# A long-convolution prologue: filter sums moved in place to GpSimd, unit sums moved to VectorE, weight conversion begun earlier, and a reordered group loop

## The chip, the cores and the metric

The kernel runs on one core of a Trainium2 chip. The metric is the device time of one execution in microseconds (us), lower being better. Each kernel was run several times, and its median is given with the lowest and the highest run. All executions quoted here are in the fast state: none is over 1.5% above the fastest of its kernel. A profile shows a single one of these executions, and executions differ by some microseconds among themselves.

## The reference, cut to what matters

```python
# B=4, S=12544, D=128, DFF=768
h_filt = (np.maximum(pos_emb @ w1, 0.0) @ w2) * window      # perceptron that makes the filter
u = x * v
y = irfft(rfft(u, 2*S) * rfft(h_filt, 2*S))[:, :S]          # long convolution along the sequence
x = (x * y).reshape(B * S, D)
h = np.maximum(np.maximum(x @ moe_w1, x @ moe_w2), x @ moe_w3)   # moe weights arrive as float64
return h @ moe_w_out
```

The Fourier transforms are done as matrix products in three stages.

## The kernel before

The program has a prologue of some 412 us and a main loop of some 2090 us. The main loop (the other three batches, the inverse transform and the feed-forward products) is bound by TensorE and is not touched. The prologue has these stages:

1. A perceptron makes the filter's taps (to 44.8 us). ScalarE, VectorE and TensorE work in turn.
2. The filter's first transform, 16 "quads" (44.8 to 69.3 us).
3. The first transform of batch 0, in 16 pairs of "units" (69.3 to about 179 us). Each unit is a product `ut = x*v`, four transposes, a quad of 32 matmuls, and a sum and a difference of its two planes.
4. A loop over 45 groups (about 184 to 379 us). Each step makes one part of the filter's spectrum (`s_second`, copied to G, then `s_filter`, copied to `ht`), multiplies it with the spectrum of batch 0, transforms back (`g_third`), and stores the tile `zs` to DRAM.
5. A hand-over to the main loop.

Two jobs run beside stage 3. The float64 weights are turned into float32 by 96 integer steps on VectorE ("conversion steps"), and the filter's own sums over its two planes are made.

```python
def over_w(ps, dst, tmp):                # sums of a unit: ScalarE copies one plane, VectorE sums
    v = by_r(ps)
    nc.scalar.copy(tmp, v[:, :, 1, :])
    for c, op in enumerate((ALU.add, ALU.subtract)):
        nc.vector.tensor_tensor(out=dst[:, :, c, :].rearrange("p k s -> p s k"), in0=tmp,
                                in1=v[:, :, 0, :], op=op)          # in1 is in PSUM

def over_w_there(ps, dst, tmp):          # the same with the sums on GpSimd
    v = by_r(ps)
    nc.scalar.copy(tmp, v[:, :, 1, :])
    d0, d1 = (dst[:, :, c, :].rearrange("p k s -> p s k") for c in range(2))
    nc.scalar.copy(d0, v[:, :, 0, :])
    nc.gpsimd.tensor_tensor(out=d1, in0=tmp, in1=d0, op=ALU.subtract)
    nc.gpsimd.tensor_tensor(out=d0, in0=tmp, in1=d0, op=ALU.add)

def filter_over_w(k):                    # sums of the filter, five blocks a call
    s0, s1, t = specH[:, k:k + 5, 0], specH[:, k:k + 5, 1], misc[:, 0:5 * FO].rearrange(...)
    nc.gpsimd.tensor_tensor(out=t, in0=s1, in1=s0, op=ALU.subtract)
    nc.gpsimd.tensor_tensor(out=s0, in0=s1, in1=s0, op=ALU.add)
    nc.scalar.copy(s1, t)

for u in range(0, NU, 2):                # the pairs of units; NU = 32
    t = uts.pop(u)
    for v in range(2):
        if u + 4 < NU:
            u_mul(u + 4 + v)             # ut = x*v on VectorE
        at = 4 * (u + v)
        quad([t[:, 4 * v + i] for i in range(4)], f1[:], spec[:, :, :, at:at + 4],
             over_w_there if (u + v) % 5 in (1, 3) else over_w)
        if at < 4 * N1 // 5:
            filter_over_w(5 * at // 4)
        some(1)                          # one conversion step
    if u + 4 < NU:
        turn2(u + 4)                     # transposes of a later pair, copied to uT by ScalarE
    ...                                  # loads of later units
    some(2)

# ---- the loop over groups; NK = 45
def g_pair(g):
    dt = zss[g]
    zs = cvp.tile([P, 2, 2, D], FP32, tag="z", name="zs", bufs=2)
    for a, op in enumerate((ALU.add, ALU.subtract)):
        nc.vector.tensor_tensor(out=zs[:, a], in0=dt[:, 0:2, :], in1=dt[:, 2:4, :], op=op)
    zss[g] = zs

def g_store(b, g):                       # 256 KB, issued by GpSimd
    nc.gpsimd.dma_start(zd[b][2 * g:2 * g + 2].rearrange(...), zss.pop(g)[:].rearrange(...))

for s in range(-1, NK + 5):              # conditions on s at the ends are cut
    s_filter(s)                          # TensorE from G; ScalarE copies to ht
    g_second(s)                          # TensorE: spectrum of the data
    g_swap(s)                            # ScalarE: xs
    g_re(s)                              # VectorE: xt
    s_second(s + 1)                      # TensorE, then ScalarE copies to G (two buffers)
    g_turn(s - 3)                        # ScalarE on dt
    g_third(s - 2)                       # TensorE: transform back, reads table wi
    wi[s] = load_dir(s, 1)               # 256 KB table, on the queue of the loads (SyncE)
    g_im(s)                              # VectorE: xs
    g_sum(s)                             # GpSimd: xt + xs
    wf[s + 4] = load_dir(s + 4, 0)       # 256 KB table, the same queue
    g_pair(s - 3)                        # VectorE: dt -> zs
    g_over_c(s - 2)                      # VectorE: ps -> dt
    g_store(0, s - 4)                    # GpSimd issues it behind its sum
```

## Time and profile before

| stage of the profiled run (us) | before |
|---|---|
| unit transform, from the filter's end to VectorE's last sum | 69.3 to 178.8 |
| first `ht` copy of the group loop | 184.09 |
| last `ht` copy of the group loop | 378.75 |
| span | 2501.8 |
| median of the first 3 runs (lowest to highest) | 2501.19 (2498.59 to 2505.18) |

The profile names an instruction by engine, line and tile: `DVE` is VectorE, `ACT` ScalarE, `POOL` GpSimd, `PE` TensorE, `PEld` its weight loads, `SP` SyncE. `zs<-dt` means that `zs` is written from `dt`. A line of the waits reads "engine, tile and line, `<-` what it waited for: us in total, times, longest us". A line of the timeline or of the chain starts with the start in us and the duration in us. Where one tile is marked as the releaser, it is the event that came last by the profile; a coincidence can be named instead of the cause. Line numbers shift between kernels: `zs` is made at L471 before and at L462 after.

The lines of the profile that carry the argument stand in the prediction, below. The whole unit stage shows no full engine; over the loop no engine is above 81%.

### The profile page before, as it was taken

Reading aid. Unit: us, or ns where it says so; the run is one execution under the profiler, and the core shown is the slowest. Engines: PE = TensorE matmul, PEld = TensorE weight load, DVE = VectorE, ACT = ScalarE, POOL = GpSimd, SP = SyncE. Lnnn points to the kernel's source line nnn. Section 1 sums busy time; section 2 is a strip of 40 time slices with the busy share of each in tenths; the row PEclk is TensorE's granted clock in tenths of the full one; section 3 lists DMA queues with packets and bytes.
Section 4 is the critical chain, followed back from the end, with each engine's and each line's share of the span. In section 5 each row is a group of like instructions: output and inputs, shape, how many; then the busy total and the mean of one; then the engine's idle time right before and its main releaser. Section 6 shows DMA issues by size and latency. Waiting matters only on the chain.

```text
span 2501.8 us, 73325 instructions
## 1 busy us (share of the span) xinstructions
PE 2344.5 (94%) x29745; PEld 1651.8 (66%) x29745; DVE 1562.3 (62%) x2969; ACT 1109.3 (44%) x2371; POOL 1528.2 (61%) x1746
## 2 busy tenths in 40 slices
PE   8678877999999999999999999999999999999998
PEld 8567765676666666776666666676666666666665
DVE  4567765666666765776777775766877673333333
ACT  2448873554444443554444443554444442222222
POOL 1656753656666666665666666665666575555555
PEclk9779998999999999999999999999999999999999
DMA  6437885987778755997878856987878753222231
GB/s 152 116 74 228 252 243 139 185 171 195 197 200 216 204 149 131 199 169 203 212 212 217 215 143 148 191 178 199 215 209 216 208 141 91 51 67 60 54 73 20
DMA packets 455227, 408.98 MB, mean 163 GB/s; under 512 B 327132, under 2 KB 331375, under 8 KB 454889
## 3 DMA queue, kind: packets, MB, share of 16 engines
q1 hardware_dynamic: 422240, 315.25, 53.5%
q0 software_dynamic: 32064, 87.60, 11.7%
q8 instruction: 234, 3.83, 0.7%
q10 hardware_dynamic: 585, 1.45, 0.3%
q14 instruction: 104, 0.85, 0.1%
HBM read 295.87 MB, written 84.67 MB: 152 GB/s over the span
## 4 chain that ended last, share of the span: by engine, by line
PE 73%; DVE 7%; ACT 4%; DMA 4%; issue 3%; POOL 0%; SPq 0%; DVEq 0%; ACTq 0%; POOLq 0%
PE ops L617 19%; PE pb L131 18%; PE pa L131 18%; PE ps L131 9%; PE ps L140 5%; PE yps L131 4%; DVE zs L471 3%; DMA zd<-zs 2%; DVE dt L456 2%; ACT hid L568 1%; DVE xs L437 1%; DMA hd<-ht 1%; ACT xs L426 1%; ACT xs L425 1%; ACT dt L464 1%
## 5 line engine op out<-in xcount | busy, mean ns | idle before, releaser
L571 DVE TENSOR_TENSOR hid<-hid,pb 128x392 f32<-128x392 f32 x768 | 429.2, 559 | 479.5 <-PE pb L131 365.9
L131 PE MATMUL pb<-gt,w_sb 128*64 128x392 f32 x3072 | 639.9, 494 | 32.5 <-ACT hid L568 32.3
L131 PE MATMUL pa<-gt,w_sb 128*64 128x392 f32 x3072 | 640.6, 495 | 11.0 <-DVE hid L571 11.0
L568 ACT ACTIVATE hid<-pa 128x392 f32<-128x392 f32 x768 | 380.4, 497 | 590.6 <-PE pa L131 565.9
L131 PEld LDWEIGHTS pb<-gt,w_sb 128*64 128x64 f32 x3072 | 218.6, 137 | 328.4 <-issue 247.8
L639 POOL DMA_DIRECT2D out_dram<-o x256 | 161.8, 636 | 292.4 <-ACT hid L568 139.4
L440 POOL TENSOR_TENSOR xt<-xt,xs 128x512 f32<-128x512 f32 x180 | 234.7, 1304 | 168.4 <-DVE xs L437 129.6
L617 PE MATMUL ops<-hid,wo_sb 128*64 128x196 f32 x3072 | 331.4, 329 | 1.4 <-DVE hid L571 1.4
L471 DVE TENSOR_TENSOR zs<-dt 128x256 f32<-128x256 f32 x360 | 290.0, 845 | 42.2 <-DMA zd<-zs 35.6
L617 PEld LDWEIGHTS ops<-hid,wo_sb 128*64 128x64 f32 x3072 | 222.3, 137 | 137.6 <-issue 116.0
L587 POOL TENSOR_TENSOR s<-hid 128x392 f32<-128x392 f32 x192 | 200.9, 1047 | 146.0 <-DVE hid L571 132.7
L587 POOL TENSOR_TENSOR s<-hid,s 128x392 f32<-128x392 f32 x192 | 199.6, 1040 | 92.6 <-DVE hid L571 91.7
L154 DVE TENSOR_TENSOR spec<-tmp,ps 128x180 f32<-128x180 f32 (+1 forms) x422 | 172.3, 503 | 110.6 <-ACT tmp L152 110.1
L587 POOL TENSOR_TENSOR hid<-hid,s 128x392 f32<-128x392 f32 x192 | 198.7, 1039 | 43.2 <-DVE hid L571 24.1
L131 PEld LDWEIGHTS pa<-gt,w_sb 128*64 128x64 f32 x3072 | 199.3, 137 | 34.1 <-DVE hid L571 10.6
L140 PE MATMUL ps<-f,uT 98*64 98x90 f32 x4096 | 203.6, 253 | 9.7 <-DVE dt L456 4.2
L140 PEld LDWEIGHTS ps<-f,uT 98*64 98x64 f32 x4096 | 191.3, 146 | 21.6 <-issue 9.7
L587 POOL TENSOR_TENSOR hid<-hid 128x392 f32<-128x392 f32 x192 | 200.4, 1059 | 0.5
L131 PE MATMUL ps<-spec,wt 128*64 128x128 f32 x2880 | 192.5, 276 | 5.7 <-DVE spec L154 2.9
L558 DVE TENSOR_TENSOR gt<-yps,xT 128x392 f32<-128x392 f32 x128 | 72.3, 565 | 200.3 <-PE ops L617 155.1
L131 PE MATMUL ps<-xt,wt 128*64 128x128 f32 x2880 | 189.8, 274 | 3.7 <-issue 2.1
L131 PEld LDWEIGHTS ps<-spec,wt 128*64 128x64 f32 x2880 | 163.2, 138 | 16.4 <-DVE dt L456 4.6
(104 smaller groups left out, 3220.0 us busy)
## 6 DMA issues: line engine op xcount, KB each, us to landing
wt<-wt_const SPq DMA_DIRECT2D x360, 256.0 KB, 5.1
ht<-hd SPq DMA_DIRECT2D x270, 256.0 KB, 4.7
zd<-zs POOLq DMA_DIRECT2D x180, 256.0 KB, 4.3
zt<-zd SPq DMA_DIRECT2D x256, 180.0 KB, 4.0
ut<-in_xr_dram SPq DMA_DIRECT2D x128, 196.0 KB, 3.7
ut<-in_vr_dram SPq DMA_DIRECT2D x128, 196.0 KB, 3.9
xT<-in_x_dram SPq DMA_DIRECT2D x512, 49.0 KB, 3.0
out_dram<-o POOLq DMA_DIRECT2D x256, 98.0 KB, 3.8
```

The source lines that it names most:

```text
L131: nc.tensor.matmul(out[64 * h:64 * h + 64], lhsT[:, 64 * h:64 * h + 64], rhs, start=start, stop=stop, skip_group_check=True)
L140: nc.tensor.matmul(ps[64 * c:64 * c + 64, 256 * i + r * N1:256 * i + (r + 1) * N1], a[:, r, :], table[:, r, c * N1:(c + 1) * N1], start=(i ...
L154: nc.vector.tensor_tensor(out=dst[:, :, c, :].rearrange("p k s -> p s k"), in0=tmp, in1=v[:, :, 0, :], op=op)
L440: nc.gpsimd.tensor_tensor(out=xts[g][:], in0=xts[g][:], in1=xss.pop(g)[:], op=ALU.add)
L456: nc.vector.tensor_tensor(out=dt[:, w:w + 4:2 + w, :] if w == 0 else dt[:, 1:5:3, :], in0=c0, in1=c1[:], op=op)
L471: nc.vector.tensor_tensor(out=zs[:, a], in0=dt[:, 0:2, :], in1=dt[:, 2:4, :], op=op)
L558: nc.vector.tensor_tensor(out=g[:].rearrange("d (w t) (m a) -> d w t m a", w=2, a=2), in0=y, in1=xT.rearrange("d w t (m a) -> d w t m a", ...
L568: nc.scalar.activation(h[:], pa[:, 0:N], Relu)
L571: nc.vector.tensor_tensor(out=h[:], in0=h[:], in1=pb[:, 0:N], op=ALU.max)
L587: nc.gpsimd.tensor_tensor(out=out[:], in0=a[:], in1=b[:], op=op)
L617: nc.tensor.matmul(ps[64 * c:64 * c + 64, 0:H2], w, rhs[:, H2 * c:H2 * c + H2], start=start, stop=True, skip_group_check=True)
L639: nc.gpsimd.dma_start(dst[64 * m:64 * m + 64, 64 * c + 2 * i:64 * c + 2 * i + 4, b, :], t[m][64 * c:64 * c + 64].rearrange("d k (q n) -> d ...
```

## The change

The intent is to shorten stage 3 by taking the sums of units off GpSimd and the second copy off ScalarE, to let GpSimd do the filter's sums undisturbed, to begin the conversion earlier, and to have G ready earlier in the loop.

```diff
-    def over_w_there(ps, dst, tmp):
-        ...
-    def u_mul(u):
+    def u_mul(u, eng=nc.vector):
         a, v = us[u]
-        nc.vector.tensor_tensor(out=a, in0=a, in1=v, op=ALU.mult)
+        eng.tensor_tensor(out=a, in0=a, in1=v, op=ALU.mult)
...
-    def filter_over_w(k):
-        s0, s1, t = specH[:, k:k + 5, 0], specH[:, k:k + 5, 1], misc[...]
-        nc.gpsimd.tensor_tensor(out=t, in0=s1, in1=s0, op=ALU.subtract)
+    def filter_over_w(k, n):
+        s0, s1 = specH[:, k:k + n, 0], specH[:, k:k + n, 1]
         nc.gpsimd.tensor_tensor(out=s0, in0=s1, in1=s0, op=ALU.add)
-        nc.scalar.copy(s1, t)
+        nc.gpsimd.tensor_single_scalar(s1, s1, 2.0, op=ALU.mult)
+        nc.gpsimd.tensor_tensor(out=s1, in0=s1, in1=s0, op=ALU.subtract)
...
             mlp_out(i - 1)                       # perceptron stage
+        if i > 1:
+            some(2)
...
             if u + 4 < NU:
-                u_mul(u + 4 + v)
+                u_mul(u + 4 + v, nc.gpsimd if v else nc.vector)
             at = 4 * (u + v)
-            quad(..., over_w_there if (u + v) % 5 in (1, 3) else over_w)
-            if at < 4 * N1 // 5:
-                filter_over_w(5 * at // 4)
+            quad(..., over_w)
             some(1)
+        if u < 30:
+            filter_over_w(3 * u, 6)
...
     for s in range(-1, NK + 5):
+        if s + 1 < NK:
+            s_second(s + 1)
         if 0 <= s < NK:
             s_filter(s)
             ...
             g_re(s)
-        if s + 1 < NK:
-            s_second(s + 1)
```

More of the change, by code (lines that the diff above doesn't have):

```diff
@@ L155, in over_w @@
                                     in1=v[:, :, 0, :], op=op)
-    def over_w_there(ps, dst, tmp):
-        v = by_r(ps)
-        nc.scalar.copy(tmp, v[:, :, 1, :])
-        d0, d1 = (dst[:, :, c, :].rearrange("p k s -> p s k") for c in range(2))
-        nc.scalar.copy(d0, v[:, :, 0, :])
-        nc.gpsimd.tensor_tensor(out=d1, in0=tmp, in1=d0, op=ALU.subtract)
-        nc.gpsimd.tensor_tensor(out=d0, in0=tmp, in1=d0, op=ALU.add)
     def as_it_is(ps, dst):
@@ L704, in quad @@
             how(ps, dst, tmp[:])
-    def filter_over_w(k):
-        s0, s1, t = specH[:, k:k + 5, 0], specH[:, k:k + 5, 1], misc[:, 0:5 * FO].rearrange(
-            "p (k f) -> p k f", k=5)
-        nc.gpsimd.tensor_tensor(out=t, in0=s1, in1=s0, op=ALU.subtract)
+    def filter_over_w(k, n):
+        s0, s1 = specH[:, k:k + n, 0], specH[:, k:k + n, 1]
         nc.gpsimd.tensor_tensor(out=s0, in0=s1, in1=s0, op=ALU.add)
-        nc.scalar.copy(s1, t)
+        nc.gpsimd.tensor_single_scalar(s1, s1, 2.0, op=ALU.mult)
+        nc.gpsimd.tensor_tensor(out=s1, in0=s1, in1=s0, op=ALU.subtract)
     warm_up(60)
@@ L748 @@
             if u + 4 < NU:
-                u_mul(u + 4 + v)
+                u_mul(u + 4 + v, nc.gpsimd if v else nc.vector)
             at = 4 * (u + v)
-            quad([t[:, 4 * v + i] for i in range(4)], f1[:], spec[:, :, :, at:at + 4],
-                 over_w_there if (u + v) % 5 in (1, 3) else over_w)
-            if at < 4 * N1 // 5:
-                filter_over_w(5 * at // 4)
+            quad([t[:, 4 * v + i] for i in range(4)], f1[:], spec[:, :, :, at:at + 4], over_w)
             some(1)
+        if u < 30:
+            filter_over_w(3 * u, 6)
         if u + 4 < NU:
```

## The prediction

> **What bounds the kernel now.** I read the page's row of slices first, then busy time by stretch, then the waits and the timeline inside the stretch that the change edits, then the chain of waits in the loop after it. The page shows TensorE 94% busy over the span, with a dip in the first sixth only. The change edits only that part (the prologue, up to about 412 us), so the question is what the prologue loses where. Busy time by stretch, with columns engine by engine, then the granted TensorE clock, the DMA share and GB/s:
>
> ```profile
> 44.80:69.30 24.50, 24.16 (x574) 23.43 (x576) 18.09 (x49) 22.90 (x19) 6.63 (x12) 1.00 0.74 181
> 69.30:148.00 78.70, 49.68 (x672) 43.90 (x668) 44.25 (x73) 26.71 (x51) 53.92 (x56) 0.74 0.45 108
> 148.00:178.80 30.80, 24.43 (x424) 21.68 (x424) 26.05 (x46) 16.50 (x27) 13.05 (x11) 0.89 0.24 55
> 188.00:388.00 200.00, 157.87 (x3204) 137.57 (x3196) 142.31 (x267) 154.39 (x311) 134.05 (x175) 0.98 0.78 237
> ```
>
> The columns after the length are TensorE, weight load, VectorE, ScalarE, GpSimd. In 44.8 to 69.3 us the filter is transformed: TensorE and ScalarE are full. From 69.3 us the units of data are transformed, in 16 pairs. The first nine pairs, which also carry the filter's sums, take 78.7 us, **8.74 us a pair, with no engine above 69%**; the last seven take 30.8 us, 4.4 us a pair. The first nine are bound by a circle of waits, not by an engine. The waits from 69 to 191 us (total, times, longest):
>
> ```profile
> ACT specH L712 <- POOL specH L711: 47.6, 18, 5.3
> DVE spec L154 <- ACT tmp L152: 44.1, 13, 6.8
> POOL spec L163 <- ACT spec L162: 35.6, 13, 6.3
> PE pst L357 <- DVE ut L352: 29.7, 13, 5.4
> ```
>
> Read them as one circle. ScalarE's copy of the filter difference (L712) waits for GpSimd; behind it in ScalarE's order stands the copy of the next unit out of PSUM; VectorE's sums wait for that copy; the next product ut stands behind those sums, and TensorE's transposes wait for it. GpSimd in turn waits for ScalarE's second copy (L162). The timeline at one such pair also shows a second thing:
>
> ```profile
> 115.20 1.07 POOL L711 TENSOR_TENSOR specH<-specH 128x320 f32<-128x320 f32 x1
> 115.47 1.40 DVE L154 TENSOR_TENSOR spec<-tmp,ps 128x360 f32<-128x360 f32 x2
> ...
> 119.33 1.20 POOL L164 TENSOR_TENSOR spec<-tmp,spec 128x360 f32<-128x360 f32 x1
> 119.38 1.56 DVE L352 TENSOR_TENSOR ut<-ut 128x392 f32<-128x392 f32 x1
> ```
>
> A VectorE sum out of PSUM takes its usual 0.70 us beside a GpSimd sum, while a VectorE product of two SBUF tiles, 0.56 us elsewhere, takes 1.56 us and ends 0.41 us after the GpSimd sum ended.
>
> In the loop over groups (188 to 388 us, 45 steps, about 4.5 us each) the waits name TensorE's s_filter matmuls for G, 29.9 us in 41 waits, and VectorE's zs for the store of zs, 35.6 us in 28. The chain of waits there runs through the second:
>
> ```profile
> 271.54 0.78 issue
> 272.33 4.27 DMA zd<-zs
> ...
> 276.72 0.77 DVE zs L471 x2
> ...
> 278.34 0.60 DVE xt L432
> 278.94 0.61 DVE xs L437
> ...
> 279.71 0.44 POOL xt L440
> 280.15 0.78 issue
> ```
>
> One turn of that ring, 271.54 to 280.15, is 8.61 us for two steps (zs has two buffers); other turns are 8.25. G isn't on it. Only the first eight steps, 3.84 to 3.88 us each by the starts of the ht copies, run on the G recurrence instead.
>
> **What the Trainium skill says.** *SBUF — State Buffer*, section "Who interferes with whom": VectorE and GpSimd share a port pair under an exclusive lock; a VectorE instruction with two SBUF inputs, or a one-input one in a two-port mode, is held by a GpSimd instruction that reads SBUF, while one with at most one SBUF input outside those modes is not. The timeline above agrees on both. *GPSIMD Engine Reference*, section 4.1: two-input elementwise work is about twice as slow as on VectorE, one-input roughly at line rate. The trace agrees on the first: 392 elements take 1.04 to 1.06 us on GpSimd and 0.56 us on VectorE; it has no f32 one-input operation on GpSimd. *TensorE: Matmul & The Clock Gate*, section "What's actually happening": after an idle window of some 3.4 us the clock halves. The trace agrees: 64 matmul records of a pair take 2.70 us in some late pairs and 4.96 us at 137.33, after transposes that had waited 3.35 us; the granted clock is 0.74 in the nine early pairs.
>
> **The change part by part, with its costs.**
>
> (a) over_w_there goes. 13 quads a run were summed on GpSimd, 2 x 1.30 = 2.6 us each, 33.8 us of GpSimd, with a ScalarE copy of 0.80 us each, 10.4 us. They become 26 VectorE sums out of PSUM at 0.70 us: +18.2 us of VectorE, 1.1 us a pair, which the lock doesn't touch.
>
> (b) The filter's sums become add, double, subtract in place, all on GpSimd. 18 x (0.93 + 0.90) = 33 us go; 15 calls of 384 elements come. From 0.86 us for 320 and 1.05 for 392, a two-input one should take 1.03; the doubling 0.5 to 1.0 us is my estimate. So 15 x about 2.7 = 40 us. What matters: **L712 leaves ScalarE, and with it the circle**. GpSimd now depends only on the filter's spectrum and on loaded units, so it can run ahead.
>
> (c) One product of each pair goes to GpSimd: 14 x 1.05 = 15 us there, 14 x 0.48 (start to start) off VectorE. GpSimd has 2.7 + 1.05 = 3.8 us a pair.
>
> (d) 14 of the 96 conversion steps move into the perceptron stage. There VectorE is busy 1.29 us of each 2.34 us, waiting for TensorE; two steps of 0.36 us fit into the remaining 1.05 us. No time is lost there, and 38 steps instead of 52 remain after 69.3 us. The filter's transform itself gains nothing (TensorE and ScalarE bound).
>
> (e) s_second goes first in each step, so that G is ready a step earlier. In the first eight steps ScalarE's own work (1.02 + 0.59 + 0.58 + 0.37 + 0.61 + 0.37 = 3.54 us) becomes the limit: some 0.25 us saved in each, 2 us. Behind them the zs ring, which doesn't contain G, stays. I allow 1 us more for the irregular steps after 320 us and take 0.6 off for the first step, which now starts with a second s_second: 2.4 us.
>
> The sum for the units. An early pair on VectorE: four sums 2.8, one product 0.48, four conversion steps 4 x 0.39 = 1.55, together 4.8 us. Its five lock-bound instructions meet a GpSimd that is busy for 3.8 of some 6 us; the 17 products of the early pairs now lose 0.28 us each (mean 0.833 against 0.556). I take 0.25 each: +1.2. So 6.0 us a pair; TensorE with 2.7 + 1.3 us a pair fits. Nine pairs: 54 us against 78.7, **saving 25**. Late pairs: VectorE 3.6 us, TensorE 4.0 plus hand-overs, 4.2 against 4.4: 1.4 us. At the end the last GpSimd sum ran until 181.6 us, 2.8 us past VectorE's last, and G waited for it: some 2.5 us gone. Sum: 25 + 1.4 + 2.5 + 2.4 = 31 us, so 2501 - 31 = **2470 us**. The 2090 us after the prologue are untouched.
>
> **Rivals.**
>
> R1, the lock replaces the circle. GpSimd may run ahead without a pause, and then each of the five VectorE instructions can wait for a whole 1.03 us sum: 4.8 + 3 to 4 = 8 us a pair, and little is saved (10 us in all, 2491). For it: four of the five stand in a row, and neighbours in the trace (118.11, 119.38) did lose 1.0 us each. Against: GpSimd's 3.8 us a pair can't fill 8 us, it is held by the loads (a unit's buffer comes free only three pairs earlier) and twice by a load of weights that waits for VectorE. My 6.0 us lies between.
>
> R2, everything flows. With few lock waits and VectorE at 4.8 us, early pairs take 5 us: 9 us more saved, 2461. TensorE then never goes idle long enough for the clock to fall.
>
> R3, the loop gains more than I say. If the G wait (29.9 us) were the real limit, up to 20 us would go: about 2452. Against it stands the chain, where G is absent from 212 to 300 us, and the DMA share of 0.78, which leaves the stores little room to land sooner.
>
> R4, the loads become the bound: 803 KB a pair at 108/0.45 = 240 GB/s are 3.4 us, below 6.0; unlikely.
>
> **Range and chances.** R1 in full gives 2491, R2 and half of R3 together some 2452. I take 2456 to 2487 for 8 in 10. Faster by over 2% means below 2451, which needs both R2 and R3: 0.05. Slower by over 2% has no mechanism here: 0.01.
>
> **What would show it.** Right, if the last sum of units ends near 152 us instead of 179; the waits of ScalarE for GpSimd in that stretch vanish; sums out of PSUM stay at 0.70 us while conversions and products are stretched by 0.2 to 0.3 us; the granted clock rises from 0.74; the ht copies are about 3.6 us apart for the first steps and 4.1 to 4.5 after, with DMA zd<-zs still in the chain and the wait of sps for G gone. Wrong, if early pairs stay near 8 us with VectorE stretched (R1), if a GpSimd doubling takes well over 1 us and TensorE waits for GpSimd's product, or if the loop shortens by over 10 us (R3).

## The result, and the profile after

| | before | after |
|---|---|---|
| median, us (lowest to highest, runs) | 2502.53 (2498.59 to 2505.18, 4) | 2480.64 (2474.94 to 2485.31, 4) |
| ratio to before (95% interval) | | 0.9913 (0.9887 to 0.9939) |
| first `ht` copy, profiled run | 184.09 | 154.20 |
| last `ht` copy | 378.75 | 356.62 |
| from there to the end | 2123.05 | 2126.9 |
| span of the profiled run | 2501.8 | 2483.5 |

A ratio is the mean time of one kernel's fast runs over that of the other's of the same rounds, so it is not quite the ratio of the medians quoted. The change saves 22 us by the medians, 0.9%. That is within the predicted range; the time lies 11 us above the predicted point. The profiled run was the slowest of the four of after.

The table already shows that two parts have opposite signs. At the first `ht` copy the new kernel is 29.9 us ahead; the loop then takes 7.8 us more, and 3.8 us go after it.

Busy time by stretch of the kernel after: early pairs (until the first sum of the nineteenth unit), late pairs, loop. The columns are TensorE, weight load, VectorE, ScalarE, GpSimd, granted clock, DMA share, GB/s.

```profile
71.50:126.50 55.00, 40.25 (x649) 36.70 (x646) 54.55 (x81) 17.41 (x28) 48.93 (x44) 0.85 0.58 140
126.50:150.70 24.20, 22.08 (x446) 20.41 (x442) 22.11 (x36) 11.06 (x18) 16.84 (x15) 0.98 0.30 72
154.20:356.60 202.40, 162.21 (x3160) 141.92 (x3160) 133.37 (x254) 147.45 (x303) 129.29 (x170) 0.95 0.72 226
```

And the loop of the kernel before in the same view:

```profile
184.10:378.70 194.60, 156.39 (x3154) 136.34 (x3156) 136.21 (x255) 152.36 (x304) 129.20 (x170) 0.98 0.78 236
```

The early pairs, where before no engine was above 69%, are now full on VectorE: 54.55 of 55.00 us. In the late pairs TensorE is at 91% and VectorE too. The loop does the same work as before, at a lower DMA share (0.72 for 0.78), in 7.8 us more.

The waits of the unit stage after, from 71 to 150 us, by total:

```profile
ACT uT L685 <- PE pst L348: 24.2, 14, 4.1
ACT tmp L152 <- PE ps L140: 21.6, 27, 1.6
PE pst L348 <- DVE ut L343: 14.8, 8, 3.2
...
DVE spec L154 <- ACT tmp L152: 7.7, 4, 5.8
```

No wait of ScalarE for GpSimd is left. VectorE's waits for ScalarE's copy fell from 44.1 us to 7.7 (both stretches hold the whole unit stage of their kernel). ScalarE now simply waits for TensorE, and TensorE in part for VectorE's product: the order of an engine-bound stage.

A piece of one early pair, from the timeline of the kernel after:

```profile
100.37 0.99 POOL L702 TENSOR_TENSOR specH<-specH 128x384 f32<-128x384 f32 x1
100.53 1.04 DVE L211 TENSOR_SCALAR tb<-tb 128x384 int32<-128x384 int32 x1
101.32 1.12 POOL L343 TENSOR_TENSOR ut<-ut 128x392 f32<-128x392 f32 x1
101.50 1.37 DVE L343 TENSOR_TENSOR ut<-ut 128x392 f32<-128x392 f32 x1
...
102.79 1.41 DVE L154 TENSOR_TENSOR spec<-tmp,ps 128x360 f32<-128x360 f32 x2
```

A conversion step, 0.36 to 0.39 us when alone, takes 1.04 us and ends at 101.57, after GpSimd's sum ended at 101.36. A VectorE product of 0.56 us takes 1.37 us beside GpSimd's product. The two sums out of PSUM, 1.41 us for both, keep their 0.70 us each.

The new GpSimd operations in that stage (60 to 155 us), with count, total and mean ns:

```profile
L701 POOL TENSOR_SCALAR specH<-specH 128x384 f32<-128x384 f32 x15 | 18.9, 1258 | 1.3
L702 POOL TENSOR_TENSOR specH<-specH 128x384 f32<-128x384 f32 x15 | 15.2, 1016 | 1.2
```

The doubling, with one input, takes 1.26 us on the mean (1.17 us by the median), more than the two-input difference of the same 384 elements.

In the loop, the chain of waits of the kernel after still goes around the ring of `zs`:

```profile
181.43 5.55 DMA zd<-zs
...
187.11 0.77 DVE zs L462 x2
...
190.11 0.43 POOL xt L431
190.54 0.84 issue
191.38 4.04 DMA zd<-zs
```

From one issue (180.65, just ahead of these lines) to the next (190.54) are 9.89 us for two steps. The prediction's turns before were 8.61 and 8.25. The stores of this piece land after 5.55 and 4.04 us. This is how the stores of the loop land by the median (DMA issues, 190 to 350 us: tile, queue, count, KB each, us from issue to landing), before and then after:

```profile
zd<-zs POOLq DMA_DIRECT2D x33, 256.0 KB, 3.8
```

```profile
zd<-zs POOLq DMA_DIRECT2D x34, 256.0 KB, 4.4
```

So three questions were open: which part of the change opened the circle in the units; what GpSimd's lock costs there now; and why the loop got longer where it had been predicted to get shorter.

### The profile page after: what moved, and what is told of

Read it like the earlier page. It is cut to its first block, busy times and chain, and to the rows that moved or that the text cites. A ratio compares the mean times of both kernels' runs of the same rounds, so it can differ in the third digit from the quotient of the medians.

```text
span 2483.5 us, 73306 instructions
## 1 busy us (share of the span) xinstructions
PE 2343.1 (94%) x29745; PEld 1651.9 (67%) x29745; DVE 1571.6 (63%) x2981; ACT 1091.4 (44%) x2340; POOL 1532.1 (62%) x1743
## 4 chain that ended last, share of the span: by engine, by line
PE 73%; DVE 7%; ACT 4%; DMA 4%; issue 3%; POOL 1%; SPq 0%; DVEq 0%; ACTq 0%; POOLq 0%
PE ops L608 19%; PE pb L131 19%; PE pa L131 18%; PE ps L131 8%; PE ps L140 4%; PE yps L131 4%; DVE zs L462 3%; DMA zd<-zs 3%; DVE dt L447 2%; ACT hid L559 1%; DVE xs L428 1%; ACT dt L455 1%; DVE hid L562 1%; ACT dt L454 1%; DMA ht<-hd 0%
## 5 line engine op out<-in xcount | busy, mean ns | idle before, releaser
L154 DVE TENSOR_TENSOR spec<-tmp,ps 128x180 f32<-128x180 f32 (+1 forms) x448 | 190.3, 521 | 73.9 <-ACT tmp L152 73.0
L578 POOL TENSOR_TENSOR hid<-hid,s 128x392 f32<-128x392 f32 x192 | 199.1, 1042 | 42.7 <-DVE hid L562 23.6
L140 PE MATMUL ps<-f,uT 98*64 98x90 f32 x4096 | 196.3, 248 | 9.9 <-DVE dt L447 4.5
L140 PEld LDWEIGHTS ps<-f,uT 98*64 98x64 f32 x4096 | 184.0, 142 | 21.0 <-issue 8.1
```

Of the source, the lines that this page charges most:

```text
L140: nc.tensor.matmul(ps[64 * c:64 * c + 64, 256 * i + r * N1:256 * i + (r + 1) * N1], a[:, r, :], table[:, r, c * N1:(c + 1) * N1], start=(i ...
L578: nc.gpsimd.tensor_tensor(out=out[:], in0=a[:], in1=b[:], op=op)
```

## The experiments

**Theory of the units (T1).** As predicted: the link that mattered was ScalarE's copy of the filter's difference (L712). Rival (T2): it was the sums of units on GpSimd, `over_w_there`, with their own copies on ScalarE.

**Theory of the loop (T3).** The new place of `s_second` makes the loop longer, by shifting the table loads ahead of the store of `zs`, so that the store lands later. Rival (T4): the loop is unequal by chance or by its earlier start, and the order is innocent.

The twelve runs in one table. The loop is from the first to the last `ht` copy in the profiled run. "Lead" is the median time at which the nearest loads of tables were issued, relative to the issue of the `zs` store: minus is ahead of the store. "Landing" is the median of the stores, 190 to 350 us.

| kernel | order of loop | median (lowest to highest, runs) | ratio to before (95%) | loop | lead | landing |
|---|---|---|---|---|---|---|
| before | old | 2502.53 (2498.59 to 2505.18, 4) | | 194.7 | +0.44 | 3.8 |
| after | new | 2480.64 (2474.94 to 2485.31, 4) | 0.9913 (0.9887 to 0.9939) | 202.4 | -0.53 | 4.4 |
| a_again | new | 2478.96 (2472.35 to 2484.07, 6) | 0.9901 (0.9885 to 0.9918) | 202.2 | -0.52 | 4.6 |
| old_loop | old | 2470.74 (2467.31 to 2472.45, 4) | 0.9873 (0.9856 to 0.9890) | 192.1 | +0.43 | 3.7 |
| new_loop_only | new | 2513.15 (2504.72 to 2518.60, 7) | 1.0041 (1.0025 to 1.0056) | 202.7 | -0.53 | 4.7 |
| held_loads | new | 2474.62 (2470.13 to 2479.13, 4) | 0.9875 (0.9861 to 0.9890) | 194.8 | +0.42 | 3.6 |
| zs3 | new | 2450.93 (2447.52 to 2453.87, 4) | 0.9794 (0.9779 to 0.9808) | 174.0 | -0.55 | 4.7 |
| zs3_old | old | 2453.71 (2447.18 to 2462.28, 5) | 0.9785 (0.9771 to 0.9799) | 177.6 | +1.05 | 3.6 |
| a_only | old | 2480.99 (2475.78 to 2486.57, 5) | 0.9904 (0.9889 to 0.9918) | 193.6 | +0.44 | 4.0 |
| b_only | old | 2503.18 (2497.28 to 2510.37, 14) | 0.9985 (0.9973 to 0.9998) | 198.1 | +0.33 | 4.0 |
| no_filter_sums (wrong on purpose) | new | 2468.75 (2463.87 to 2469.96, 4) | 0.9849 (0.9828 to 0.9869) | 199.4 | -0.52 | 4.2 |
| no_early_conv | new | 2491.35 (2484.05 to 2493.60, 4) | 0.9938 (0.9915 to 0.9961) | 196.3 | -0.52 | 4.4 |
| store_sp | new | 2443.40 (2441.27 to 2449.99, 5) | 0.9755 (0.9733 to 0.9777) | 173.8 | | 4.4 |
| best | new | 2445.28 (2439.65 to 2450.36, 5) | 0.9769 (0.9749 to 0.9788) | 172.7 | | 4.5 |

All are correct but no_filter_sums. The medians of before in the later rounds were between 2503.8 and 2506.4, so ratios are safer to compare than medians.

### The loop

**a_again** is the kernel after, once more, unedited.

> The changed kernel once more, for a second profile and for a time from the same rounds as the others. In its first profile the loop over groups took 202.4 us from the first to the last ht copy against 194.7 before, although the prediction gave it 2.4 us of gain. Theory O (the order itself makes the loop slower): here too 200 us or more. Theory C (chance in how the transfers meet): anywhere from 190 to 203. Ratio to before 0.991 +- 0.003 in both.

Measured: 0.9901, and a loop of 202.2 us against 202.4. The long loop is no accident of one profile.

**old_loop** is the kernel after with the old order of the loop.

```diff
-        if s + 1 < NK:
-            s_second(s + 1)
         if 0 <= s < NK:
             s_filter(s)
             ...
             g_re(s)
+        if s + 1 < NK:
+            s_second(s + 1)
```

> The changed kernel with the loop's old order (the filter's second transform behind the data's). Theory O: the loop takes 193 to 196 us again, the kernel is 6 to 9 us faster than the changed one. Theory C: within 3 us of the changed one in time, and the first eight steps are 2 us longer.

Measured: 0.9873, some 7 us faster than a_again by the ratios, and a loop of 192.1 us. The wait of `sps` for G is back, and that costs nothing. From the waits of old_loop, 190 to 350 us:

```profile
DVE zs L462 <- DMA zd<-zs: 30.4, 26, 2.7
PE sps L799 <- ACT G L786: 25.4, 33, 1.2
```

and from those of the kernel after in the same stretch, where the second line no longer stands among the first ones:

```profile
DVE zs L462 <- DMA zd<-zs: 37.7, 23, 4.6
```

The prologue up to the first `ht` copy (152.86 us) is as good as that of after. The gain of the change is thus in the units, and the new order takes part of it away.

**new_loop_only** is the kernel before with the new order alone (the same edit as in the change).

> The kernel before with the loop's new order alone. Theory O: 5 to 9 us slower than before (ratio 1.002 to 1.004). Theory C and the prediction: 0 to 3 us faster than before (ratio 0.999 to 1.000). In both its units take 109 us as before, and the waits of sps for G are gone.

Measured: 1.0041 (1.0025 to 1.0056), about 10 us slower than before, with a loop of 202.7 us. T4 falls: the order alone makes the loop 8 us longer, at whatever time it starts. Its first eight steps took 31.2 us (before 31.9), its other 36 took 171.5 us (before 162.7): the early steps gain a little, as predicted, and the later ones lose more.

The table shows the link in all runs with two buffers and the loads left as they were. Five kernels of the new order have a lead of about -0.5 us and landings of 4.2 to 4.7 us; four of the old order have +0.3 to +0.4 us and 3.7 to 4.0 us. The loops are 196.3 to 202.7 us and 192.1 to 198.1 us, so single loops overlap, but the landings do not. The reason for the lead is in the order of instructions: the buffer of `wi` is released by `g_third`, which in the new order comes earlier relative to the GpSimd sum behind which the store is issued. Two loads of 256 KB are then under way when the store begins.

**held_loads** tests just this. In the new order it makes the two loads of a step wait for the sum, through a transfer of 512 bytes that reads `xt` on the queue of the loads.

```diff
-                wi[s] = load_dir(s, 1)           # behind g_third
...
             g_sum(s)
+            nc.sync.dma_start(mark[s], xts[s][0:1, 0, 0, :])
+            if s >= 2:
+                wi[s] = load_dir(s, 1)
             if s + 4 < NK:
                 wf[s + 4] = load_dir(s + 4, 0)
```

> The changed kernel, new order, two zs buffers, but the two 256 KB table loads of each step are held back until the sum that also releases the store of zs: a store of one row of that sum, on the loads' own queue ahead of them. In the traces the loads are issued 0.53 us ahead of the store of zs in the new order and 0.43 us behind it in the old one, and the store's time to landing is 4.4 to 4.6 us against 3.7. Theory L (the loads now stand ahead of the store): the store lands in 3.7 us again, the loop takes 190 to 195 us and the kernel is 7 to 12 us faster than the changed one. Rival B (TensorE waits for the buffers that over_c frees, whatever the loads do): the loop stays at 199 to 204 us.

Measured: the lead became +0.42 us, the landing fell to 3.6 us, and the loop to 194.8 us, with the new order of instructions. The time, 0.9875, is that of old_loop. So the order acts through the sequence of transfers, as T3 says. There is a price: TensorE now waits for the tables. From the waits of held_loads, 190 to 350 us:

```profile
DVE zs L463 <- DMA zd<-zs: 34.7, 25, 4.0
PE ps L132 <- DMA wt<-wt_const: 21.4, 19, 2.5
```

**zs3** and **zs3_old** take the ring away, by a third buffer of `zs`, in the new and in the old order. A third buffer did not fit at first (29.94 KB a partition for 28.75); the last units' `tmp` was put into the buffers of G to make room, in both runs. The diff is shortened to what matters.

```diff
-        zs = cvp.tile([P, 2, 2, D], FP32, tag="z", name="zs", bufs=2)
+        zs = cvp.tile([P, 2, 2, D], FP32, tag="z", name="zs", bufs=3)   # in the prologue
```

> The changed kernel with three zs buffers in the loop over groups instead of two (the temporary of the last unit sums shares two other buffers to make room). If the ring of two zs buffers with its store is what sets the loop's step, as the prediction says, the waits of zs for its store (42.8 us) nearly vanish and the step goes from 4.6 us toward 3.7 to 4.1: 20 to 35 us faster than the changed kernel. If the DMA engines are the real limit (share 0.70 to 0.78 here), or the two ht buffers take over, the wait moves to the ht copies or the loads and less than 10 us is gained.

> Three zs buffers and the loop's old order. With two zs buffers the old order was 8 us faster than the new one (loops of 192.1 and 202.2 us). If the loop is then held by the circle of ht, xs, G and the filter's matmuls, which the new order takes out, its steps are 3.84 to 3.87 us and the loop takes 176 to 182 us: 2 to 8 us slower than the 174.0 of three buffers with the new order, so that the order's sign turns round. Rival: the new order costs the loop something whatever the buffers; then this is faster than the new order with three buffers, 165 to 170 us.

Measured: 0.9794 and 0.9785, loops of 174.0 and 177.6 us. From the waits of zs3, 190 to 350 us:

```profile
DVE zs L467 <- DMA zd<-zs: 1.6, 2, 1.0
```

The wait of 37.7 us is gone, although its stores still land after 4.7 us. The ring of two buffers was what bound the loop in both orders. Whether the new order is better once the ring is gone is not settled: the profiled loop is 3.6 us shorter, but the ratios overlap and lean the other way.

### The units

**a_only** is the kernel before with the sums of every unit on VectorE, and nothing else. The filter's sums keep their copy on ScalarE.

```diff
-                 over_w_there if (u + v) % 5 in (1, 3) else over_w)
+                 over_w)
```

> The kernel before, with one thing of the change: every unit's sums out of PSUM on VectorE. The filter's sums keep their copy on ScalarE. Theory S (that copy, ScalarE waiting for GpSimd, closes the circle, as the prediction says): the early pairs stay above 7.5 us and at most 10 us is gained. Rival G (the unit sums on GpSimd and their second ScalarE copy close it): early pairs of 6 to 6.5 us, 17 to 25 us gained.

**b_only** is the kernel before with the filter's sums in place on GpSimd, and nothing else.

```diff
-        nc.gpsimd.tensor_tensor(out=t, in0=s1, in1=s0, op=ALU.subtract)
         nc.gpsimd.tensor_tensor(out=s0, in0=s1, in1=s0, op=ALU.add)
-        nc.scalar.copy(s1, t)
+        nc.gpsimd.tensor_single_scalar(s1, s1, 2.0, op=ALU.mult)
+        nc.gpsimd.tensor_tensor(out=s1, in0=s1, in1=s0, op=ALU.subtract)
```

> The kernel before, with one thing of the change: the filter's sums in place on GpSimd, without the copy on ScalarE, in the 18 calls of 320 elements of before. Two in five units are still summed on GpSimd. Theory S: the circle is open and 15 us or more is gained, unless GpSimd, which now has 2 x (0.86 + 1.0 + 0.86) + 0.8 x 2.6 = 7.5 us a pair, has become the bound. Rival G: nothing gained (within 4 us of before), since GpSimd's unit sums now stand behind three filter operations instead of two and the units wait for them.

Measured: a_only 0.9904, first `ht` copy at 159.16 us, 24.9 us earlier than before. b_only 0.9985, first `ht` copy at 183.75 us, 0.3 us earlier. T2 stands: taking the sums of units off GpSimd is enough, with L712 left where it was. (Whether the GpSimd sums or their second ScalarE copy mattered more was not separated.) b_only alone doesn't decide T1. L712 has left ScalarE there, but three GpSimd operations have come for two, and what its expectation feared came true: GpSimd is full, 74.28 of 78.00 us, for 53.05 in the kernel before.

```profile
69.00:147.00 78.00, 51.13 (x738) 44.53 (x733) 63.49 (x84) 23.31 (x37) 74.28 (x74) 0.78 0.50 120
```

So ScalarE's copies wait for the sums of units on GpSimd instead. From its waits, 69 to 185 us:

```profile
DVE spec L154 <- ACT tmp L152: 32.1, 13, 7.7
...
ACT tmp L152 <- POOL spec L164: 21.1, 4, 6.8
POOL spec L163 <- ACT spec L162: 17.7, 5, 7.2
```

In a_only L712 is still on ScalarE and still waits for GpSimd, but GpSimd, no longer held by sums of units, is soon done, and VectorE is now the full engine (53.84 us of 55.60, 68.4 to 124 us). From its waits, 68 to 156 us:

```profile
ACT specH L712 <- POOL specH L711: 13.6, 10, 2.2
```

The total is 13.6 us where before it was 47.6, and the longest is 2.2 us where it was 5.3.

**no_filter_sums** measures the cost of the lock by itself. It is the kernel after without the filter's sums, so GpSimd has only its products in the unit stage. Its result is wrong on purpose (relative error 0.517).

```diff
-        if u < 30:
-            filter_over_w(3 * u, 6)
```

> The changed kernel without the filter's sums on GpSimd (its output is wrong on purpose). It measures what these sums cost VectorE through the shared port. The prediction put 1.2 us a pair of lock waits on the nine early pairs, its rival R1 3 to 4 us. Without 3.3 us of GpSimd work a pair, and with GpSimd's one product a pair left, the early pairs should fall from 6.1 us to about 5.0 to 5.3 (VectorE's 4.8 us plus the rest) if the prediction is right, a kernel 7 to 10 us faster; to 4.8 or less, with more than 12 us gained, if the lock costs more than I said; and stay at 6.1 if something else holds them.

Measured: the transposes of nine pairs are 44.8 us apart for 55.7 us in the kernel after: 4.98 us a pair for 6.19. So the filter's sums cost VectorE 1.2 us a pair (1.05 us if one measures from the filter's end to the end of the eighteenth unit's sums). The busy time of the same stretch, first of no_filter_sums and then of a_again:

```profile
71.00:125.00 54.00, 43.68 (x818) 39.68 (x816) 53.42 (x96) 21.80 (x35) 11.72 (x11) 0.97 0.72 172
```

```profile
71.00:125.00 54.00, 36.95 (x641) 33.62 (x640) 53.58 (x80) 17.37 (x27) 47.91 (x43) 0.91 0.59 143
```

VectorE is as full in both, but gets through 96 instructions instead of 80 in the same 54 us, and TensorE through 818 matmul records instead of 641.

**no_early_conv** is the kernel after without the 14 conversion steps in the perceptron stage, so 52 instead of 38 fall into the units.

```diff
-        if i > 1:
-            some(2)
```

> The changed kernel without the 14 conversion steps in the perceptron stage: 52 instead of 38 of them then stand beside the units. By the prediction each costs VectorE 0.39 us plus some 0.25 us of lock wait: 9 us slower, with early pairs for 13 pairs instead of 9. If VectorE is not the bound of the units, 0 to 3 us slower.

Measured: 0.9938 for 0.9901 to 0.9913. The units took 90.9 us (68.33 to 159.20) for 79.1 to 80.3 in the two profiles of after: about 11 us more, 0.78 us for each of the 14 steps, twice what a step takes alone. The stage began 1.7 to 3.2 us earlier, so the first `ht` copy (162.79 us) is 9 to 10 us later than in those two, and the times differ by 6 to 9 us. The loop was 6 us shorter in this profile than in those of after; why is open, and single loops move by some microseconds.

This run also tells what the rest is worth. Up to the loop it is a_only with the filter's sums in place and one product of each pair on GpSimd. From the filter's end to VectorE's last sum it takes 91.2 us, for 87.6 in a_only (one profile each; the two of after differ by 1.2). So these two parts gained nothing in the units on top of a_only, and rather cost some 3.6 us; what after has there beyond a_only comes from the early conversion steps. In total time a_only, one edit, equals the whole change: 0.9904 for 0.9901 to 0.9913.

### A version that beats both

**store_sp** shortens the ring without a third buffer. The store is issued right behind `g_pair`, on the queue of the loads, and no longer waits for GpSimd's next sum. The queue and the place change together; their shares are not separated.

```diff
-        nc.gpsimd.dma_start(zd[b]...)
+        (nc.sync if b == 0 else nc.gpsimd).dma_start(zd[b]...)
...
             g_pair(s - 3)
+            g_store(0, s - 3)
...
-        if 0 <= s - 4 < NK:
-            g_store(0, s - 4)
```

> The changed kernel, two zs buffers, with the store of zs issued on the loads' queue right behind the differences that make it, instead of on GpSimd's queue behind the next step's sum. The ring of two buffers then loses VectorE's next step, GpSimd's sum and the 0.78 us of issue: from 8.25 us and more for two steps to about 0.8 + 0.8 + 0.5 + 4.4 = 6.5 us. If the ring is what holds the loop, it takes 172 to 180 us, as with three buffers, and the kernel is 22 to 30 us faster than the changed one. If the store now delays the loads (it stands ahead of them in the same queue and waits for VectorE), the loop takes 190 us or more.

Measured: 0.9755 (0.9733 to 0.9777), correct, 2.4% faster than before and the fastest kernel of the study. The loop took 173.8 us. The stores land after 4.4 us as in the kernel after, but nothing waits for them any more (0.4 us in all). Busy time of store_sp:

```profile
190.00:290.00 100.00, 91.01 (x1828) 77.86 (x1820) 94.19 (x154) 84.78 (x180) 58.09 (x75) 0.98 0.94 274
```

VectorE is 94% busy and the steps are a constant 3.80 us. The sum and difference for `zs` take 1.83 us together there, since they meet GpSimd's sum; that is the next thing to look at.

**best** adds 16 conversion steps in the filter's transform to store_sp, in the hope of taking more off the units.

```diff
-        some(2 if u < 2 and k < 2 else 3)
+        some((2 if k < 2 else 3) if u < 2 else 5)
```

> The kernel with the store of zs on the loads' queue, and 16 more of the conversion steps in the second half of the filter's transform, where VectorE waited 5.8 us idle for the first unit in every profile so far. 22 instead of 38 steps are left beside the units. Taking 14 steps away from the units saved 11 us (0.78 us each, lock wait included), so 16 more should save 8 to 12 us: 2432 to 2436 us, the last unit sum near 139 to 142 us instead of 150. If the steps only delay the start of the units, or their inputs aren't loaded in time, the gain is under 4 us.

Measured: 0.9769, no gain over 0.9755. The timeline of best shows why:

```profile
67.03 0.36 DVE L202 TENSOR_SCALAR ta<-raw 128x384 int32<-128x384 int32 x1 [2.94 <-DMA raw<-in_moe_w_dram]
...
77.89 1.39 DVE L154 TENSOR_TENSOR spec<-tmp,ps 128x360 f32<-128x360 f32 x2
```

VectorE reached weights that were not loaded yet and waited 2.94 us, and the steps behind them held the first sums of units back to 77.89 us, for 70.99 in store_sp. The units ended 2.1 us earlier (147.60 for 149.73), and the total shows none of it.

## Why the prediction was right or wrong

The time was right: 2480.64 us in a range of 2456 to 2487, and "within 2%", as given 0.94. In part this is luck: the link named as decisive was not, and the loop went the other way; the sum held because the change removed the decisive link too. The parts, in the profiled run, with a saving as plus:

| step of the prediction | predicted | measured | from |
|---|---|---|---|
| start of the units (the filter's end) | 0 | -1.9 | 69.3 to 71.2 |
| nine early pairs (to the end of the eighteenth unit's sums) | +25 | +25.6 | 78.6 to 53.0 |
| seven late pairs | +1.4 | +4.5 | 31.0 to 26.5 |
| hand-over to the loop | +2.5 | +1.8 | 178.8 to 184.09, then 150.68 to 154.20 |
| loop | +2.4 | -7.8 | 194.7 to 202.4 |
| from the last `ht` on | 0 | -3.8 | 2123.05 to 2126.9 |
| sum | 31 | 18.3 | span 2501.8 to 2483.5 |

- **Early pairs: right in size.** 5.9 us a pair by the ends of the sums, 6.2 by the transposes, for the predicted 6.0. The lock's term, +1.2 us a pair, was met by no_filter_sums (1.05 to 1.2), more exactly than its working deserves: that term stood for all of the lock, and what was measured is of the filter's sums alone, while GpSimd's product was left in. The products on VectorE lost 0.48 us each (1.034 us for 0.556) where 0.25 had been taken, and GpSimd was busy 5.4 us a pair (48.93 us in nine), not 3.8.
- **Early pairs: wrong in cause.** The step that failed reads "L712 leaves ScalarE, and with it the circle". a_only keeps L712 and gains 24.9 us before the loop. b_only takes L712 off ScalarE and gains 0.3 us, though with GpSimd full in its place; and no_early_conv, which moves L712 away without filling GpSimd's queue with sums of units, is no shorter in the units than a_only. All parts but the loop's order together (old_loop) gain 31.2 us there, so what the others add to a_only is 6.3 us. The largest total in the list of waits was a place where the circle showed, not the link that had to go. The third line of that list (GpSimd's L163 for ScalarE's L162) named the sums of `over_w_there`, and their removal was enough. The prediction removed both links in one sum, so the size did not suffer.
- **Late pairs: mis-sized.** 3.8 us a pair for 4.2 (the last transposes are 3.64 us apart). The prediction took 4.0 us for TensorE and added hand-overs; the transposes took 1.05 to 1.08 us in place of 1.3, and with 2.70 us for the matmuls nothing was left over. That is a flow bound by engines, which R2 had expected of the early pairs; there VectorE at 5.9 us a pair did not allow it.
- **Doubling on GpSimd: mis-sized.** 1.17 us by the median, above the estimated 0.5 to 1.0 us. It cost nothing further, because VectorE set the pace.
- **R1** did not come: GpSimd was 89% busy in the early pairs, and VectorE still met the filter's sums with a loss of 1.05 to 1.2 us a pair and not 3 to 4.
- **Loop: the step that failed.** "Behind them the zs ring, which doesn't contain G, stays" was true of the waits and false of the length. The ring was taken as a constant of 8.25 to 8.61 us a turn. Its largest term, the landing of the store, depends on which transfers are issued just before it, and the new order put 512 KB of loads there. new_loop_only (+0.41%) and held_loads (loop back to 194.8 us) show it. The first eight steps did gain, 1.9 us in this profile (31.9 to 30.0), near the predicted 2; the other 36 lost 9.7 (4.79 us a step, where 4.1 to 4.5 had been named as a sign). R3, a larger gain in the loop, had no part in it.
- **Still open.** The units began 1.9 us later in the profiled run of after, and (d) had said that no time is lost before them. In that run the first 96 matmul records of the filter's transform took 5.59 us for 3.94 before; in a_again it took 3.94 us and the whole stage was the shortest of all, and b_only, without early steps, has the 5.59 us too, so this is chance. But there is a second sign: the filter's transform began at 43.7 to 45.4 us in the nine profiles with early conversion steps, and at 42.5, 42.7, 43.1, 44.2 and 44.9 us in b_only, no_early_conv, a_only, new_loop_only and before, which have none. The means differ by 1.3 us and the ranges overlap, so the early steps may cost the perceptron stage 1 to 2 us of the 11 that they save later; this isn't settled. The stretch after the loop varies from 2117 to 2130 us over the profiles without a pattern that we could name; the 3.8 us above are within it.

## What to carry to other kernels

When a list of waits forms a circle, name the link by removing one at a time: the largest total need not be the one that has to go. Here removing the one with the largest total gained 0.15% of the time and another 0.96%. Look at what each removal puts in its place: the first filled GpSimd, so it tested less than it seemed to. When an instruction is moved, ask which buffers it frees earlier and so which transfers it sends ahead of another: a ring that ends in a store grows with that store's landing, and here the landing depended on its neighbours. Where such a ring bounds a loop, issue the store at once behind its producer before giving it another buffer: that took 28 us off the loop here, as much as a third buffer did, at no memory.

## What the Trainium skill lacked or had wrong

- *GPSIMD Engine Reference*, section 4.1 "Engine selection", has one-input work on GpSimd as roughly line-rate and only two-input work as slow. Here a one-input TENSOR_SCALAR of 384 float32 a partition took 1.17 us by the median (1.26 us mean), more than the two-input TENSOR_TENSOR of the same size at 1.00 to 1.02 us. For this form the measurement differs, and decides.
- *DMA: Bandwidth & Descriptors*, section "Issuing engines are not separate DMA queues", says that transfers of several engines interleave on the same 16 DMA engines and that issuing from more of them saves sequencer time alone. The runs agree that they interleave. What it lacks is the price in landing time: two 256 KB loads issued 0.5 us ahead of a 256 KB store instead of 0.4 us behind moved its landing from 3.7 to 4.0 us to 4.2 to 4.7 us, and a loop by 8 us. It also lacks the other side of the choice of issuer: behind a busy GpSimd's sum the store was issued late, and issuing it on SyncE, right behind its producer, shortened the loop from 202 to 173.8 us.
- *SBUF — State Buffer*, section "Who interferes with whom", has the lock right: products and conversion steps were held, sums with one input out of PSUM were not (0.70 us before and after). Beyond two slowdowns from single measurements, it gives no size for a stream of such instructions beside a busy GpSimd: here 14 more conversion steps of 0.39 us lengthened the stage by 0.78 us each, and the filter's sums cost 1.05 to 1.2 us for each pair with five VectorE instructions of the kind that is held.
